# Transposing softmax probabilities on VectorE in 32 by 32 blocks instead of on TensorE, in a chunked attention fused with a squared-ReLU MLP

## The chip, the cores and the metric

The kernel runs on one core of a Trainium2 chip. The metric is device time in microseconds (us) of one launch; the time before is 877.12 us, the median of three runs (876.96 to 877.26).

The engines are named as in the profile: PE is TensorE's matmul stream and PEld its weight loads, DVE is VectorE, ACT is ScalarE, POOL is GpSimd, and SP is the engine that issues most DMAs.

## The reference

Attention is local: 8 batches by 8 heads, 576 positions, head size 64, cut into chunks of 64 positions that attend only within themselves. Its output, 4608 tokens by 512, feeds an MLP with a hidden size of 2048. All is float32.

```python
scores = (1/8) * q_c @ k_c.T            # per chunk: 64 x 64
attn = exp(scores - max(scores)); attn = attn / (sum(attn) + 1e-9)
x = attn @ v_c                          # gathered to tokens x 512
r = maximum(x @ w_in, 0)
out = (s * r * r + b) @ w_out
```

## The kernel before, in words

**Tiles.** The 4608 tokens are 36 tiles of 128. An MLP block (`Layer`) is four tiles, 512 tokens, so there are nine blocks; the attention for a block is done as two groups (`Attention`) of N = 2 tiles each. The hidden size is 16 slices of 128 (NJ = 16). Every float32 operand of the MLP is split into a high and a low part (`xh`/`xl`, `gh`/`gl`, and both halves of the weights), and each product is three matmuls.

**The steady loop** (lines 386 to 425) runs over j = 0 to 17 in every block. Step j issues `up(j)` (line 256, 12 matmuls 128x512 into one of two `ps_h` banks), then `square(j)` and `bias(j)`: ACT's relu (L263), DVE's product (L264, called the square here), ACT's `gh` (L269), DVE's `gl` (L270). Then comes `down(j-2)` (line 281, 12 matmuls into four `ps_o` banks): `LAG` is 2. `ps_h` has two buffers, so `up(j+2)` needs `gl(j)` done; `down(j)` needs both `gh(j)` and `gl(j)`.

**Attention inside the loop.** While block b's MLP runs, the attention of block b+1 is worked in at fixed places. `attention_plan` maps a place (j, phase) to steps: phase 0 stands ahead of `up(j)`, phase 1 behind it, phase 2 between `square(j)` and `bias(j)`. Every engine takes its instructions in this order; nothing reorders them (`manual_schedule`). A group has a base step n, 1 for the first and 9 for the second:

- (n-1, 0) loads, (n, 1) scores on PE (L171), (n, 2) maximum on DVE (L176)
- (n+1, 2) subtraction on DVE (L181), (n+2, 0) exp on ACT (L186), (n+2, 2) sum on DVE (L190)
- (n+4, 0) `norm`: three DVE instructions (L193 to L195)
- (n+5, 1) `transposes`: 8 PE transposes of 128x128 into PSUM (L202)
- (n+6, 0) `copies`: two ACT copies 128x512 from PSUM to `pT` (L207)
- (n+6, 1) `values`: 64 small matmuls with `pT` as the moving operand (L215)
- (n+7, 0) `x_hi` on ACT (L226), (n+7, 2) `x_lo` on DVE (L230); `x` is read by `up(0)` of the next block.

The scores, the transposes and the values take turns in one `ps_a` buffer of two PSUM banks. `p`, `pT`, `m` and `z` have one buffer each.

The attention of the first block is done in a prologue (lines 319 to 383), where the weights are also unpacked; `attention_plan(4)` supplies the second block's attention during the first block. The last block has no attention beside it. So `attention_plan` runs eight times, 16 groups in all, of which 14 have `tb` of 8 or more.

Of the kernel before, what the change touches and what calls it, by code (L numbers as in the profile page):

```python
# [1 line left out]

# [6 lines left out]
F32 = mybir.dt.float32  # L9
# [9 lines left out]
def local_attention_then_squared_relu_mlp(ctx: ExitStack, tc, qkv, w, s, b, out):  # L19


    nc = tc.nc
    P = 128
# [4 lines left out]
    NHP = H // 2  # L28
    LAG = 2
    N = 2  # L30
# [8 lines left out]
    att = ctx.enter_context(tc.tile_pool(name="att", bufs=1))  # L39
# [91 lines left out]
    class Attention:  # L131
# [65 lines left out]
        def transposes(self):  # L197
            p = self.p.rearrange("p g c k -> p g (c k)")
            self.ps = self.bank(1)
            for g in range(G):  # L200
                i, hp = divmod(g, NHP)
                nc.tensor.transpose(out=self.ps[:, i, hp * P:(hp + 1) * P], in_=p[:, g, :], identity=ident)  # L202

        def copies(self):
            pT = att.tile([P, N, NHP * P], F32, name="pT")
            for i in range(N):
                nc.scalar.copy(out=pT[:, i, :], in_=self.ps[:, i, :])  # L207
            self.pT = pT.rearrange("p i (a t) -> p i a t", a=NHP)
# [23 lines left out]
    def block(tb0, bank):  # L232
        x = [xp.tile([P, NHP, 4 * P], F32R, name=n) for n in ("xh", "xl")]
        return x, [Attention(tb0 + i, x, i * P, bank) for i in range(0, 4, N)]
# [73 lines left out]
    def attention_plan(tb0):  # L308
        x, groups = block(tb0, steady_bank)
        plan = {}  # L310
        for a, n in zip(groups, (1, 9)):
            for at, *fs in (((n - 1, 0), a.load_qk, a.load_v), ((n, 1), a.scores), ((n, 2), a.peak), ((n + 1, 2), a.sub),
                            ((n + 2, 0), a.exp), ((n + 2, 2), a.sum), ((n + 4, 0), a.norm), ((n + 5, 1), a.transposes),
                            ((n + 6, 0), a.copies), ((n + 6, 1), a.values), ((n + 7, 0), a.x_hi), ((n + 7, 2), a.x_lo)):
                plan.setdefault(at, []).extend(fs)
        return x, plan, plan.pop((0, 0))


    x, (one, two) = block(0, first_bank)
    for a in (one, two):  # L320
        a.p = wp.tile([P, 4, DM], F32, name="wp")[:, 0:2, :].rearrange("p i (g c k) -> p (i g) c k", g=NHP, c=2)
    next_x, plan, (load_next_qk, load_next_v) = attention_plan(4)
    pair = [Pair(k) for k in range(NJ)]
    one.load_qk()
# [61 lines left out]
    for tb0 in range(0, NTB, 4):  # L386
# [39 lines left out]
        previous, x, plan, loads = layer, next_x, {}, ()  # L426
        if tb0 + 4 < NTB:
            layer = Layer(tb0 + 4, x)
        if tb0 + 8 < NTB:
            next_x, plan, loads = attention_plan(tb0 + 8)  # L430
# [33 lines left out]
```

## Time and profile before

| | us |
|---|---|
| median of three runs | 877.12 (876.96 to 877.26) |
| the profiled execution's own time | 877.19 |
| its span (first to last instruction) | 875.4 |
| PE busy | 860.9 (98%) |
| DVE busy | 375.7 (43%) |
| ACT busy | 309.3 (35%) |
| POOL busy | 42.1 (5%) |
| mean granted TensorE clock | 0.998 of full |

The span plus 1.8 us makes the execution's own time. A matmul's busy time overlaps that of its neighbours, so the time of a matmul stream is read from start to start. The first block ends near 115 us of the span; from there on the eight others repeat one pattern.

### The profile page before, as it was taken

The numbers are of one execution on the slowest core, as the hardware profiler recorded it, in microseconds if no ns is written. First come the engines' busy times: TensorE is split into PE (matmuls) and PEld (weight loads), VectorE is DVE, ScalarE is ACT, GpSimd is POOL, SyncE is SP. The second block draws the span as 40 slices with busy tenths as digits, with TensorE's granted clock in tenths as the row PEclk, the third lists the DMA queues.
The fourth block names the chain that finished last, engine by engine and source line by source line (L and its number), as shares of the span: only waits on it lengthen the run. The fifth ranks groups of instructions, "written<-read, shape, count | busy, mean of one in ns | idle before, by whom it ended". The sixth has DMA issues, their size and how long they took to land.

```text
span 875.4 us, 13710 instructions
## 1 busy us (share of the span) xinstructions
PE 860.9 (98%) x5986; PEld 709.1 (81%) x5986; DVE 375.7 (43%) x486; ACT 309.3 (35%) x465; POOL 42.1 (5%) x24
## 2 busy tenths in 40 slices
PE   7899999999999999999999999999999999999998
PEld 6677888888888888888888888888888888888886
DVE  6898945242434333333434252443333343423222
ACT  5777643223322332223232332233222322232222
POOL 2434300000000000000000000000000000000000
PEclk9999999999999999999999999999999999999999
DMA  8556430201210030203020212002020300010001
GB/s 340 214 180 230 145 121 1 74 1 33 89 52 22 5 116 1 73 0 121 1 73 0 71 51 72 2 25 97 1 73 1 121 0 25 1 49 1 1 0 49
DMA packets 20368, 55.41 MB, mean 63 GB/s; under 512 B 2260, under 2 KB 2516, under 8 KB 20308
## 3 DMA queue, kind: packets, MB, share of 16 engines
q1 hardware_dynamic: 20160, 54.40, 17.6%
q8 instruction: 47, 0.77, 0.3%
q10 hardware_dynamic: 148, 0.13, 0.0%
q14 instruction: 13, 0.11, 0.0%
HBM read 45.09 MB, written 9.44 MB: 62 GB/s over the span
## 4 chain that ended last, share of the span: by engine, by line
PE 87%; DVE 6%; issue 2%; DMA 2%; ACT 2%; POOL 0%; SPq 0%; ACTq 0%; POOLq 0%
PE ps_o L281 42%; PE ps_h L256 40%; PE ps_a L215 2%; PE ps_a L171 2%; DVE wp L127 2%; DMA raw<-in_w_dram 2%; PE ps_a L202 1%; DVE ps_h L264 1%; DVE f L113 1%; DVE f L111 1%; DVE g L270 1%; ACT g L269 1%; ACT f L101 0%; DMA wp<-in_qkv_dram 0%; ACT raw L105 0%
## 5 line engine op out<-in xcount | busy, mean ns | idle before, releaser
L281 PE MATMUL ps_o<-wp,g 128*128 128x512 f32 x1728 | 417.0, 392 | 0.0
L256 PE MATMUL ps_h<-xh,wp 128*128 128x512 f32 (+1 forms) x1160 | 379.9, 390 | 4.5 <-DVE g L270 3.4
L281 PEld LDWEIGHTS ps_o<-wp,g 128*128 128x128 f32 x1728 | 321.3, 188 | 66.8
L264 DVE SCALAR_TENSOR_TENSOR ps_h<-ps_h,sb,r 128x512 f32<-128x512 f32 x144 | 109.1, 758 | 412.6 <-ACT r L263 412.4
L256 PEld LDWEIGHTS ps_h<-xh,wp 128*128 128x128 f32 x1160 | 217.5, 188 | 51.8 <-DVE g L270 3.5
L256 PE MATMUL ps_h<-xl,wp 128*128 128x512 f32 (+1 forms) x580 | 225.4, 389 | 0.0
L263 ACT ACTIVATE r<-ps_h 128x512 f32<-128x512 f32 x144 | 86.1, 598 | 373.1 <-PE ps_h L256 373.1
L269 ACT ACTIVATE g<-ps_h,sb 128x512 fp32r<-128x512 f32 x144 | 99.3, 689 | 118.2 <-DVE ps_h L264 118.2
L270 DVE SCALAR_TENSOR_TENSOR g<-ps_h,sb,g 128x512 fp32r<-128x512 f32 x144 | 107.6, 747 | 68.2 <-ACT g L269 68.2
L256 PEld LDWEIGHTS ps_h<-xl,wp 128*128 128x128 f32 x580 | 109.3, 189 | 22.2
L119 POOL TENSOR_TENSOR f<-f,raw 128x1024 int32<-128x1024 int32 (+1 forms) x17 | 39.5, 2321 | 67.8 <-DVE f L113 46.0
L298 ACT COPY f<-ps_o 128x512 f32<-128x512 f32 (+1 forms) x35 | 20.4, 583 | 41.4 <-PE ps_o L281 39.1
L101 ACT ACTIVATE f<-raw 128x1024 f32<-128x1024 f32 (+1 forms) x17 | 18.6, 1092 | 11.2 <-DMA raw<-in_w_dram 10.0
L113 DVE SCALAR_TENSOR_TENSOR f<-raw,f 128x1024 uint32<-128x1024 uint32 (+1 forms) x17 | 21.9, 1286 | 0.5
L127 DVE TENSOR_TENSOR wp<-f,wp 128x1024 fp32r<-128x1024 f32 (+1 forms) x17 | 22.0, 1292 | 0.0
L230 DVE TENSOR_TENSOR xl<-ps_a,xh 128x512 fp32r<-128x512 f32 x32 | 20.5, 683 | 1.7 <-ACT xh L226 1.7
L195 DVE TENSOR_TENSOR p<-p,z 128x1024 f32<-128x1024 f32 x16 | 19.6, 1225 | 0.6
L215 PEld LDWEIGHTS ps_a<-pT,v 64*64 64x64 f32 x960 | 15.4, 134 | 5.3 <-issue 4.9
L171 PEld LDWEIGHTS ps_a<-raw 64*64 64x64 f32 x960 | 15.4, 134 | 5.3 <-issue 5.3
L123 ACT CAST wp<-f 128x1024 fp32r<-128x1024 f32 (+1 forms) x17 | 16.9, 997 | 7.6 <-POOL f L119 7.5
L186 ACT ACTIVATE p<-p 128x1024 f32<-128x1024 f32 x16 | 17.0, 1063 | 6.9 <-DVE p L181 6.9
L181 DVE TENSOR_TENSOR p<-ps_a,m 128x1024 f32<-128x1024 f32 x16 | 19.4, 1215 | 0.0
(44 smaller groups left out, 238.7 us busy)
## 6 DMA issues: line engine op xcount, KB each, us to landing
raw<-in_w_dram SPq DMA_DIRECT2D x32, 512.0 KB, 4.6
raw<-in_qkv_dram SPq DMA_DIRECT2D x30, 512.0 KB, 4.7
out_dram<-f SPq DMA_DIRECT2D x35, 256.0 KB, 2.1
v<-in_qkv_dram SPq DMA_DIRECT2D x30, 256.0 KB, 3.1
wp<-in_qkv_dram SPq DMA_DIRECT2D x6, 512.0 KB, 6.0
wp<-in_qkv_dram SPq DMA_DIRECT2D x6, 256.0 KB, 7.6
out_dram<-f ACTq DMA_DIRECT2D x1, 128.0 KB, 2.1
out_dram<-f SPq DMA_DIRECT2D x1, 128.0 KB, 2.0
```

The costliest lines, as they stand in the source:

```text
L113: nc.vector.scalar_tensor_tensor(out=u, in0=high, scalar=0x80000000, in1=u, op0=ALU.bitwise_and, op1=ALU.bitwise_or)
L119: nc.gpsimd.tensor_tensor(out=i, in0=i, in1=low.bitcast(I32), op=ALU.add)
L127: nc.vector.tensor_tensor(out=lo, in0=f, in1=hi.bitcast(F32), op=ALU.subtract)
L171: nc.tensor.matmul(out=self.ps[cols, c, i * NHP + hp, :], lhsT=qk[rows, 0, h, :], rhs=qk[rows, 1, h, :], start=True, stop=True)
L215: nc.tensor.matmul(out=ps[i if apart else 0][cols, c, i * NHP + hp, :], lhsT=self.v[i][rows, h, :], rhs=self.pT[rows, i, hp, cols], start= ...
L230: nc.vector.tensor_tensor(out=lo, in0=ps, in1=hi.bitcast(F32), op=ALU.subtract)
L256: nc.tensor.matmul(out=self.ps[j][:, cols], lhsT=w[:, c, :], rhs=x[:, c, :], start=(c == 0 and i == 0), stop=(c == NHP - 1 and i == 2))
L263: nc.scalar.activation(out=r, in_=ps, func=AF.Relu)
L264: nc.vector.scalar_tensor_tensor(out=ps, in0=ps, scalar=s_col, in1=r, op0=ALU.mult, op1=ALU.mult)
L269: nc.scalar.activation(out=gh, in_=ps, func=AF.Identity, bias=b_col)
L270: nc.vector.scalar_tensor_tensor(out=gl, in0=ps, scalar=b_col, in1=gh.bitcast(F32), op0=ALU.add, op1=ALU.subtract)
L281: nc.tensor.matmul(out=self.acc[t], lhsT=x[:, ts], rhs=w, start=(j == 0 and i == 0), stop=(j == NJ - 1 and i == 2))
```

## The change

For groups with `tb` of 8 or more, the PE transposes at (n+5, 1) and the ACT copies at (n+6, 0) are gone. In their place VectorE transposes `p` into `pT` in sixteen instructions, each on 32 partitions by 8 blocks of 32 elements (256 elements in a row), from quarter t of the tokens to quarter k of the keys. Four are at (n+4, 2), six at (n+5, 0) and six at (n+5, 2). All other steps keep their places.

```diff
+        def turn(self, blocks):
+            if blocks[0] == 0:
+                self.pT = att.tile([P, N, NHP * P], F32, name="pT").rearrange("p i (a t) -> p i a t", a=NHP)
+            p = self.p.rearrange("p g c k -> p g (c k)")
+            for n in blocks:
+                t, k = (slice(32 * b, 32 * b + 32) for b in divmod(n, 4))
+                nc.vector.transpose(out=self.pT[k].rearrange("p i a t -> p (i a) t")[:, :, t], in_=p[t, :, k])
...
-                            ((n + 2, 0), a.exp), ((n + 2, 2), a.sum), ((n + 4, 0), a.norm), ((n + 5, 1), a.transposes),
-                            ((n + 6, 0), a.copies), ((n + 6, 1), a.values), ((n + 7, 0), a.x_hi), ((n + 7, 2), a.x_lo)):
+                            ((n + 2, 0), a.exp), ((n + 2, 2), a.sum), ((n + 4, 0), a.norm),
+                            ((n + 6, 1), a.values), ((n + 7, 0), a.x_hi), ((n + 7, 2), a.x_lo)):
                 plan.setdefault(at, []).extend(fs)
+
+            if a.tb < 8:
+                turns = ((n + 5, 1), a.transposes), ((n + 6, 0), a.copies)
+            else:
+                turns = [(at, partial(a.turn, range(*r))) for at, r in (((n + 4, 2), (0, 4)), ((n + 5, 0), (4, 10)), ((n + 5, 2), (10, 16)))]
+            for at, f in turns:
+                plan.setdefault(at, []).append(f)
```

## Rows read from the trace of the kernel before

**Rows 1.** Page, part 1: busy time of each engine, share of span, instructions
```profile
PE 860.9 (98%) x5986; PEld 709.1 (81%) x5986; DVE 375.7 (43%) x486; ACT 309.3 (35%) x465; POOL 42.1 (5%) x24
```

**Rows 2.** Chain that ended last, 115 to 875 us, by line
```profile
by line: PE ps_o L281 47.6%; PE ps_h L256 45.8%; PE ps_a L215 2.2%; PE ps_a L171 2.0%; PE ps_a L202 1.6%; DVE ps_h L264 0.1%; DVE g L270 0.1%; ACT g L269 0.1%; ACT r L263 0.1%; DVE f L296 0.1%; ACT f L298 0.1%; issue 0.0%; ACTq L263 0.0%
```

**Rows 3.** Waits, 115 to 875 us: total us, times, longest us
```profile
PEld ps_a L215 <- issue: 4.9, 14, 0.4
...
PEld ps_a L215 <- ACT pT L207: 0.4, 1, 0.4
PE ps_h L256 <- DVE g L270: 0.3, 1, 0.3
```

**Rows 4.** Groups of instructions by shape: the work removed (busy us, mean ns)
```profile
L207 ACT COPY pT<-ps_a 128x512 f32<-128x512 f32 x36 | 19.2, 590 | 0.0
...
L202 PE MATMUL ps_a<-ident,p 128*128 128x128 f32 x128 | 16.5, 272 | 0.0
```

**Rows 5.** Timeline, PE, a second group, steps 13 to 15: start us, us
```profile
288.90 0.39 PE L256 MATMUL ps_h<-xh,wp 128*128 128x512 f32 x1
...
294.34 0.39 PE L256 MATMUL ps_h<-xh,wp 128*128 128x512 f32 x1
...
297.06 1.03 PE L202 MATMUL ps_a<-ident,p 128*128 128x128 f32 x8
...
297.85 2.98 PE L281 MATMUL ps_o<-wp,g 128*128 128x512 f32 x12
...
300.67 0.39 PE L256 MATMUL ps_h<-xh,wp 128*128 128x512 f32 x1
...
303.48 1.16 PE L215 MATMUL ps_a<-pT,v 64*64 64x64 f32 x64
...
312.87 0.39 PE L256 MATMUL ps_h<-xh,wp 128*128 128x512 f32 x1
```

**Rows 6.** Timeline, PE, a first group, steps 6 and 7
```profile
341.39 0.39 PE L256 MATMUL ps_h<-xh,wp 128*128 128x512 f32 x1
...
347.72 0.39 PE L256 MATMUL ps_h<-xh,wp 128*128 128x512 f32 x1
```

**Rows 7.** Timeline, DVE, the same second group, steps 13 and 14 and behind them
```profile
289.25 0.16 DVE L193 TENSOR_SCALAR z<-z 128x16 f32<-128x16 f32 x1
289.45 0.25 DVE L194 RECIPROCAL z<-z 128x16 f32<-128x16 f32 x1
289.74 1.23 DVE L195 TENSOR_TENSOR p<-p,z 128x1024 f32<-128x1024 f32 x1
292.51 0.76 DVE L264 SCALAR_TENSOR_TENSOR ps_h<-ps_h,sb,r 128x512 f32<-128x512 f32 x1 [1.55 <-ACT r L263]
294.02 0.75 DVE L270 SCALAR_TENSOR_TENSOR g<-ps_h,sb,g 128x512 fp32r<-128x512 f32 x1 [0.76 <-ACT g L269]
297.95 0.76 DVE L264 SCALAR_TENSOR_TENSOR ps_h<-ps_h,sb,r 128x512 f32<-128x512 f32 x1 [3.18 <-ACT r L263]
299.47 0.75 DVE L270 SCALAR_TENSOR_TENSOR g<-ps_h,sb,g 128x512 fp32r<-128x512 f32 x1 [0.76 <-ACT g L269]
...
306.76 1.29 DVE L230 TENSOR_TENSOR xl<-ps_a,xh 128x512 fp32r<-128x512 f32 x2 [0.21 <-ACT xh L226]
```

**Rows 8.** Busy time in one stretch: PE, PEld, DVE, ACT, POOL, PEclk, DMA share, GB/s
```profile
287.86:303.40 15.54, 15.54 (x74) 12.75 (x72) 5.33 (x8) 4.23 (x7) 0.00 (x0) 1.00 0.00 0
```

**Rows 9.** Groups of instructions by shape: DVE durations, mean ns
```profile
L230 DVE TENSOR_TENSOR xl<-ps_a,xh 128x512 fp32r<-128x512 f32 x32 | 20.5, 683 | 1.7 <-ACT xh L226 1.7
...
L195 DVE TENSOR_TENSOR p<-p,z 128x1024 f32<-128x1024 f32 x16 | 19.6, 1225 | 0.6
L181 DVE TENSOR_TENSOR p<-ps_a,m 128x1024 f32<-128x1024 f32 x16 | 19.4, 1215 | 0.0
...
L127 DVE TENSOR_TENSOR wp<-f,wp 128x512 fp32r<-128x512 f32 x2 | 1.4, 681 | 0.0
...
L296 DVE COPY f<-ps_o 128x256 f32<-128x256 f32 x1 | 0.4, 425 | 1.1 <-ACT f L298 1.1
```

More of the change, by code (lines that the diff above doesn't have):

```diff
@@ L1 @@
 from contextlib import ExitStack
+from functools import partial
 import concourse.bass as bass
```

## The prediction

> **What bounds the kernel now.** I read the busy table first: PE is busy for 98% of the span, DVE for 43% [rows 1]. A busy PE need not be the bound, so next I read the chain that ended last, cut to the part behind the first block: its five PE lines sum to 99.2% [rows 2]. The transposes, L202, are 1.6% of that chain: they are part of the bounding stream, not beside it. Then the waits of the same stretch: in 760 us PE waits for another engine in two places, 0.4 and 0.3 us, and the only wait that repeats is 0.4 us of issue ahead of each set of values [rows 3]. So behind 115 us, time taken out of PE's stream comes off the end, as long as nothing new makes PE wait. Last I read one group's timeline, on PE for what the transposes cost and on DVE for the room there is.
>
> **The change, part by part.**
>
> *Removed from PE.* The page gives a transpose a mean of 272 ns [rows 4], but these overlap: the eight start at 297.06 and the next matmul at 297.85. The full cost is read from step to step. A step without attention takes 294.34 − 288.90 = 5.44 us; the step with the transposes takes 300.67 − 294.34 = 6.33 us [rows 5]. The difference is **0.89 us**. A first group has the same 347.72 − 341.39 = 6.33 us [rows 6]. The trace has 128 such transposes, 16 groups of eight [rows 4]; two groups (tiles 4 and 6) keep theirs by the condition on `tb`, so 14 lose them: 14 × 0.89 = **12.46 us**.
>
> *Removed from ACT.* Two copies of 590 ns per group [rows 4]. ACT waits for PE in these steps, and nothing on PE waits for ACT but the values, which have a new releaser. I cost it at zero, and it brings nothing more. Likewise `ps_a`: it changes hands twice a group instead of three times, but PE shows no wait on it [rows 3].
>
> *Added to DVE.* Sixteen transposes a group, of 256 elements in a row on 32 partitions. No row shows a VectorE transpose, so I bound its start-to-start time. Going from 512 to 1024 elements adds 1225 − 681 = 544 ns, so 256 elements would take 681 − 272 = 409 ns; the one copy of 256 elements took 425 [rows 9]. Short strided rows cost nothing by themselves: the subtraction writes `p` in runs of 64 and takes 1215 ns against the 1225 of the contiguous product [rows 9]. Independent neighbours overlap: the two pieces of `x_lo` together take 1.29 us where one takes 0.683, so the second starts some 0.08 us before the first ends [rows 7, 9]. Where each waits for the one before, as the three of `norm`, there is a gap of about 0.035 us instead [rows 7]. **Low end** 0.409 − 0.08 = 0.33 us, **usual high end** 0.425 + 0.035 = 0.46 us. An end far above that: should the transposing path take each float32 at half the rate, a row of 256 would cost what 512 cost, 0.683 + 0.035 = 0.72 us. I take 0.43, the duration of the 256-element copy with neither overlap nor gap, because its shape is the nearest.
>
> *The room for it.* The first four stand behind the square of step n+4, which ends at 292.51 + 0.76 = 293.27 [rows 7]. The values need the last; they start at 303.48 now, and would at 303.48 − 0.89 = 302.59 [rows 5]. In these 9.32 us DVE also does one `gl` (0.75) and one square (0.76) [rows 7]; four hand-offs of 0.035 make 0.14. That leaves 7.67 us, so sixteen transposes fit if one takes no more than **0.48 us**. At 0.43 they take 6.9 and 0.8 us is over; at 0.46 they take 7.4 and it still fits, by 0.3. In the stretch of the group's steps DVE is busy for 5.33 of 15.54 us [rows 8], and 6.9 more makes 12.2.
>
> *What is queued behind them.* On DVE the first four hold back `gl` of step n+4: it would start at 293.27 + 4 × 0.43 = 295.0 instead of 294.02. The six at (n+5, 0) then run to 295.0 + 0.75 + 2.6 = 298.35, and the square, ready at 297.95 now, waits 0.4 us for them [rows 7]. ACT's `gh` waits with it, and the last six then put `gl` of step n+5 to 298.35 + 0.76 + 2.6 = 301.7 instead of 299.47. Who needs that `gl`? The `down` two steps later, and `up` two steps later through the two `ps_h` buffers. In a first group that `up` starts two steps of 5.44 us behind the one at 294.34's place, after the values too: near 306. It has about 3.5 us to spare. In a second group the next block's `up(0)` stands at 312.87 [rows 5], and `x_lo` ends at 308.05 [rows 7], behind steps that are unchanged; DVE has caught up by then. I cost all these at zero: their cover is the LAG of two steps. The steps bring no DMA and pass neither SP's queue nor POOL's.
>
> *Sum.* 14 × 0.89 = 12.46 us off, nothing back. The profiled execution took 877.19, giving 864.73; against the median, 0.07 lower, it is **864.7 us**.
>
> The Trainium skill speaks against the change: "VectorE: DVE Perf Modes", section "Rules for kernel authors", says to transpose 128×128 on TensorE where a PSUM destination will do. By that rule alone the 12.46 us would not be had. The rows say why it need not hold here: PE is the chain and DVE idles for 10 us of the 15.54 [rows 2, 8].
>
> **The rivals.**
>
> *A thin stall.* The room is 0.48 us each, and my bounds reach 0.46. If the sixteen never overlap, and filling a block of 32 columns first adds 32/512 of 0.544, 0.034 us, one takes 0.425 + 0.035 + 0.034 = 0.494: the values wait 16 × 0.494 − 7.67 = 0.23 us a group, 3.3 us in all, giving **868.0**. With twice the gap, 0.529, the wait is 0.8 and the time 864.7 + 11.1 = 875.8, nearly all given back. For it: consecutive transposes go to another quarter of the partitions each time, a pattern that no row shows. Against: 512-element neighbours overlap. The skill's same page, section "Two Vector instructions with no wait between them", has a rule on the side of this rival: an instruction whose output or input starts in another group of 32 partitions than the last one's begins only when all earlier ones have finished. By it none of the overlap would be had; no run here shows it yet.
>
> *VectorE becomes the bound.* At half rate, 0.72 us each, sixteen take 11.5 us: the values wait 11.5 − 7.67 = 3.85 us in each of 14 groups, 54 us, giving **918.6 us**, slower. It decides from 0.48 + 0.89/16 = 0.54 us each, where the loss meets the gain. For it: nothing shows how fast float32 is transposed. Against: every DVE row is near one element per nanosecond, whatever its pattern [rows 9].
>
> *No gain from PE.* The removed 0.89 us might reappear as a wait for something else that was hidden behind it, at **877.1**. Against: PE has no wait of any size behind 115 us, and the square chain has whole steps to spare [rows 3, 7].
>
> **How the numbers follow.** All hidden, 864.7: chance 0.68. Thin stall, up to the 875.8 of the double gap: 0.17. No gain: 0.05. DVE the bound: 0.10. The likeliest is 864.7. Below it there is only the spread of single runs and the rounding of 0.89 (0.01 × 14), so the low end is 863.9. The high end takes in the thin stall at 0.494 and most of the way to the double gap, 871.5, which leaves out the two last cases and the worst of the second, under 0.2. About 0.2%, 1.75 us, is what a measurement of this kernel can tell from no change. Faster by more than that: the first case and nearly all of the second, 0.85; within it 0.05; slower 0.10.
>
> **What would show it.** Right: sixteen PE transposes of `p` left in place of 128; steps n+5 of 5.44 us in both groups; no wait of the values on DVE; a start-to-start time of the VectorE transposes under 0.48 us; DVE's busy time up by 14 × 16 × 0.43 = 96 us, PE's chain share still 99% behind the first block. Wrong: a wait of L215 on the VectorE transposes, repeated 14 times (thin stall under 0.9 us, DVE the bound above it); or a wait of `up` on `gl` at step n+7, which would show that I misjudged the cover of two steps.

## The result and the profile after

The changed kernel takes **864.60 us** (median of four runs, 864.37 to 865.99) against 877.04 in the same comparison: a ratio of 0.9859, 95% interval 0.9847 to 0.9872, or 12.4 us less. The forecast was 864.7. The profiled execution took 864.60 too, with a span of 862.8. One execution of the version below that starts the transposes earlier ran at a mean granted clock of 0.557 and took 1419.95 us; it is left out of that version's time.

The busy table, the chain behind the first block by line, and the waits there, of the changed kernel (the lines that answer to [rows 1 to 3]):

```profile
PE 847.9 (98%) x5874; PEld 697.2 (81%) x5874; DVE 472.2 (55%) x710; ACT 295.4 (34%) x437; POOL 42.1 (5%) x24
```

```profile
by line: PE ps_o L291 48.3%; PE ps_h L266 46.5%; PE ps_a L225 2.2%; PE ps_a L172 2.0%; DVE ps_h L274 0.1%; DVE g L280 0.1%; ACT g L279 0.1%; ACT r L273 0.1%; DVE f L306 0.1%; ACT f L308 0.1%; issue 0.0%; ACTq L273 0.0%
```

```profile
PEld ps_a L225 <- issue: 4.9, 14, 0.4
...
PEld ps_a L225 <- ACT pT L217: 0.4, 1, 0.4
PE ps_h L266 <- DVE g L280: 0.3, 1, 0.3
```

PE is as full as before, over a shorter span, and DVE's busy time has risen by 96.5 us, against the 96 that I had put. The chain has lost its 1.6% of transposes and gained nothing: the four PE lines sum to 99.0%. In the waits the row to look for is one that is not there: no wait of the values, now L225, for the VectorE transposes, L212 (the ACT row is the one group that keeps its copies). The three rows of before stand unchanged.

The two shapes that replace those of [rows 4], by shape and with the mean in ns:

```profile
L212 DVE STREAM_TRANSPOSE pT<-p 32x256 f32<-32x256 f32 x224 | 97.5, 435 | 3.9
...
L203 PE MATMUL ps_a<-ident,p 128*128 128x128 f32 x16 | 2.1, 272 | 0.0
```

The timeline of a second group, steps 13 to 15, on DVE (it answers to [rows 7]) and on PE ([rows 5]):

```profile
289.71 0.76 DVE L274 SCALAR_TENSOR_TENSOR ps_h<-ps_h,sb,r 128x512 f32<-128x512 f32 x1 [1.55 <-ACT r L273]
290.38 1.77 DVE L212 STREAM_TRANSPOSE pT<-p 32x256 f32<-32x256 f32 x4
292.19 0.75 DVE L280 SCALAR_TENSOR_TENSOR g<-ps_h,sb,g 128x512 fp32r<-128x512 f32 x1
292.97 2.70 DVE L212 STREAM_TRANSPOSE pT<-p 32x256 f32<-32x256 f32 x6
295.70 0.76 DVE L274 SCALAR_TENSOR_TENSOR ps_h<-ps_h,sb,r 128x512 f32<-128x512 f32 x1
296.49 2.71 DVE L212 STREAM_TRANSPOSE pT<-p 32x256 f32<-32x256 f32 x6
299.23 0.75 DVE L280 SCALAR_TENSOR_TENSOR g<-ps_h,sb,g 128x512 fp32r<-128x512 f32 x1
```

```profile
291.54 0.39 PE L266 MATMUL ps_h<-xh,wp 128*128 128x512 f32 x1
...
296.98 0.39 PE L266 MATMUL ps_h<-xh,wp 128*128 128x512 f32 x1
...
299.79 1.16 PE L225 MATMUL ps_a<-pT,v 64*64 64x64 f32 x64
300.89 3.47 PE L291 MATMUL ps_o<-wp,g 128*128 128x512 f32 x14
```

Step 14 takes 296.98 − 291.54 = 5.44 us, as one without attention did. In a first group the same step is 343.14 − 337.70 = 5.44 us:

```profile
337.70 0.39 PE L266 MATMUL ps_h<-xh,wp 128*128 128x512 f32 x1
...
343.14 0.39 PE L266 MATMUL ps_h<-xh,wp 128*128 128x512 f32 x1
```

On DVE everything from 289.71 to 299.98 stands in one row, with gaps of at most 0.04 us. The six of 2.70 us, the last of them 0.44 long, start every (2.70 − 0.44)/5 = 0.45 us. The last transpose ends at 296.49 + 2.71 = 299.20 and the values start at 299.79: **0.59 us of room**, little more than one transpose.

### The profile page after: what moved, and what is told of

It is laid out like the page before. It is cut to its first block, busy times and chain, and to the rows that moved or that the text cites. A ratio compares the mean times of both kernels' runs of the same rounds, so it can differ in the third digit from the quotient of the medians.

```text
span 862.8 us, 13668 instructions
## 1 busy us (share of the span) xinstructions
PE 847.9 (98%) x5874; PEld 697.2 (81%) x5874; DVE 472.2 (55%) x710; ACT 295.4 (34%) x437; POOL 42.1 (5%) x24
## 4 chain that ended last, share of the span: by engine, by line
PE 88%; DVE 7%; issue 2%; ACT 2%; DMA 1%; POOL 0%; SPq 0%; ACTq 0%; POOLq 0%
PE ps_o L291 42%; PE ps_h L266 41%; PE ps_a L225 2%; PE ps_a L172 2%; DVE wp L128 2%; DVE ps_h L274 1%; DVE f L114 1%; DVE f L112 1%; DVE g L280 1%; ACT g L279 1%; DMA raw<-in_w_dram 1%; DVE z L191 0%; PE ps_h L67 0%; DVE m L177 0%; POOL f L120 0%
## 5 line engine op out<-in xcount | busy, mean ns | idle before, releaser
L212 DVE STREAM_TRANSPOSE pT<-p 32x256 f32<-32x256 f32 x224 | 97.5, 435 | 3.9
L128 DVE TENSOR_TENSOR wp<-f,wp 128x1024 fp32r<-128x1024 f32 (+1 forms) x17 | 22.0, 1294 | 0.0
L225 PEld LDWEIGHTS ps_a<-pT,v 64*64 64x64 f32 x960 | 15.4, 134 | 5.3 <-issue 4.9
L177 DVE TENSOR_REDUCE m<-ps_a 128x16 f32<-128x1024 f32 x16 | 19.4, 1215 | 0.0
```

Of the source, the lines that this page charges most:

```text
L128: nc.vector.tensor_tensor(out=lo, in0=f, in1=hi.bitcast(F32), op=ALU.subtract)
L212: nc.vector.transpose(out=self.pT[k].rearrange("p i a t -> p (i a) t")[:, :, t], in_=p[t, :, k])
L225: nc.tensor.matmul(out=ps[i if apart else 0][cols, c, i * NHP + hp, :], lhsT=self.v[i][rows, h, :], rhs=self.pT[rows, i, hp, cols], start= ...
```

## The experiments

They were run in three lots, each beside the kernel before; a ratio is against that. Each is the changed kernel with the edit shown.

**Is the VectorE work hidden? Leave it out.** `pT` is filled with a constant instead, by one memset of 0.91 us a group.

```diff
-            for n in blocks:
...
+            if blocks[0] == 0:
+                nc.vector.memset(self.pT, 1.0 / CH)
```

> The sixteen VectorE transposes of a group are left out; pT is filled once per group with 1/64 by one memset, so the values are no longer those of the softmax. Theory (the transposes are wholly hidden behind TensorE): same time as the changed kernel, 864.6 us within 0.5. Rival (they still cost something, by holding back the squares or by stalling the values a little): lower by what they cost, 861 to 863.

Measured 864.54 us, ratio 0.9854 (0.9837 to 0.987). Sixteen transposes a group, 97.5 us of DVE time in the changed kernel's profile, cost nothing that can be measured.

**Is the gain PE's stream alone? Put the PE transposes back, unread.**

```diff
             else:
+                plan.setdefault((n + 5, 1), []).append(a.transposes)
```

> The changed kernel, with the eight TensorE transposes of each of the 14 groups put back at their old place; nobody reads them, no ScalarE copies follow. Theory (the gain is TensorE's stream alone): all of it is lost, 864.6 + 14 x 0.89 = 877.1 us. Rival (part of the gain came from the ScalarE copies that are gone and from the new releaser of the values): about half comes back, 868 to 874.

Measured 877.08 us, ratio 1.0001 (0.9991 to 1.001). The whole gain is gone. The two ScalarE copies and the new releaser of the values, both as in the changed kernel, are worth nothing; the rival with half of it falls. The third turn of `ps_a` came back together with the transposes, so this run does not part those two; neither trace shows a wait on it.

**How much room is there? Do one, two or four transposes twice.** The edit with two:

```diff
+                turns[2] = ((n + 5, 2), partial(a.turn, list(range(10, 12)) + list(range(10, 16))))
```

> One of the sixteen VectorE transposes of each group done twice (17 a group). Theory (0.55 us of room, 0.45 for one more): no stall, 864.6 us, and the last transpose ends some 0.1 us ahead of the values. Rival (two extra ones cost 5.3 us by a price each, not by a room): 2.7 us more, 867.3.

> Two of the sixteen VectorE transposes of each group are done twice (18 a group), ahead of the last six. Theory (the values have 0.5 to 0.6 us of room, one transpose takes 0.45): 2 x 0.45 - 0.55 = 0.35 us of stall a group, 14 of them, 869.5 us (868.5 to 870.5), with a wait of the values on the VectorE transposes. Rival (VectorE is idle for 45% of the span, so two more fit): 864.6.

> Four of the sixteen done twice (20 a group). Theory: 4 x 0.45 - 0.55 = 1.25 us a group, 17.5 us in all, 882 us, slower than the kernel before: the point from which VectorE decides is passed. Rival (they fit): 864.6; rival that the stall is taken up in the next steps: less than twice what two extra ones cost.

Measured 864.62 us with one (ratio 0.9858, 0.9843 to 0.9873), 869.94 with two (0.9917, 0.9902 to 0.9932) and 884.03 with four (1.0081, 1.0066 to 1.0096). The first is free, the next costs 5.3 us, and four turn the change into a loss. It is a room and not a price each: 0, 5.3 and 19.4 us for one, two and four.

With one extra, the last seven on DVE and the values on PE:

```profile
296.52 3.18 DVE L212 STREAM_TRANSPOSE pT<-p 32x256 f32<-32x256 f32 x7
...
299.82 1.16 PE L225 MATMUL ps_a<-pT,v 64*64 64x64 f32 x64
```

The last ends at 299.70, 0.12 us ahead of the values. With two, the last eight on DVE, the values and the matmul behind them on PE, and the wait that was missing above:

```profile
297.41 3.65 DVE L212 STREAM_TRANSPOSE pT<-p 32x256 f32<-32x256 f32 x8
```

```profile
300.72 1.54 PE L225 MATMUL ps_a<-pT,v 64*64 64x64 f32 x64
302.19 8.50 PE L291 MATMUL ps_o<-wp,g 128*128 128x512 f32 x36
```

```profile
PEld ps_a L225 <- DVE pT L212: 2.8, 14, 0.2
```

From the start of the values to the next matmul it is 302.19 − 300.72 = 1.47 us, where the changed kernel has 300.89 − 299.79 = 1.10. The difference of 0.37, 14 times, is 5.2 us: the measured loss. The wait row alone shows 2.8, so such a loss is read from start to start. With four, on PE:

```profile
305.62 0.80 PE L225 MATMUL ps_a<-pT,v 64*64 64x64 f32 x6
307.01 1.14 PE L225 MATMUL ps_a<-pT,v 64*64 64x64 f32 x58 [0.59 <-DVE pT L212]
308.08 4.19 PE L291 MATMUL ps_o<-wp,g 128*128 128x512 f32 x17
```

Here it is 2.46 us, 1.36 more than 1.10, and 14 × 1.36 = 19.0. I had expected 1.25; the values now stop twice, six of them ahead of the second stop. Which part of that makes the 0.1 us a group was not tried.

**Do neighbours overlap? Halve the transposes.** Each becomes two of 128 elements, one per tile, in the same quarters of the partitions.

```diff
-                nc.vector.transpose(out=self.pT[k].rearrange("p i a t -> p (i a) t")[:, :, t], in_=p[t, :, k])
+                for i in range(N):
+                    nc.vector.transpose(out=self.pT[k, i, :, t], in_=p[t, i * NHP:(i + 1) * NHP, k])
```

> Each VectorE transpose is done as two of 128 elements (one for each of the two tiles), one right after the other: both halves have the same quarter of the partitions for input and for output, the next pair another output quarter. Theory H (a transpose that starts in another quarter than its predecessor starts only when that has finished; neighbours in the same quarters overlap): the second half of a pair starts about 0.08 us before the first ends, the first half of the next pair 0.02 us after the end; a pair takes some 0.54 us, 16 pairs 8.7 us instead of 7.2, and the values wait 0.9 us a group: 877 us (873 to 881). Theory N (transposes never overlap, whatever the quarter): 32 x 0.32 = 10.2 us, a stall of 2.4 us a group, 898 us. Theory O (all overlap, the quarter has no part in it): 32 x 0.23 = 7.4 us, at most 867 us.

Measured 867.27 us (ratio 0.9888, 0.9873 to 0.9902): by the time alone, theory O. The trace says H. Four cuts of the DVE timeline, each wider than the one before it, show the first one, two, three and four of a row of halves (start of the first, us to the end of the last):

```profile
294.17 0.30 DVE L213 STREAM_TRANSPOSE pT<-p 32x128 f32<-32x128 f32 x1
...
294.17 0.49 DVE L213 STREAM_TRANSPOSE pT<-p 32x128 f32<-32x128 f32 x2
...
294.17 0.81 DVE L213 STREAM_TRANSPOSE pT<-p 32x128 f32<-32x128 f32 x3
...
294.17 1.00 DVE L213 STREAM_TRANSPOSE pT<-p 32x128 f32<-32x128 f32 x4
```

All of them, with the shortest, median and longest in ns:

```profile
L213 DVE STREAM_TRANSPOSE pT<-p x448: 256/278/307, 152.3 to 764.3; 32x128 f32<-32x128 f32 x150
```

The ends come alternately 0.19 and 0.32 us apart. The shortest lasts 256 ns, so the second of a pair starts at most 0.49 − 0.26 = 0.23 into the row, 0.07 or more before the first ends at 0.30; the third, which changes the output's quarter and takes 0.30, starts some 0.02 after the second ends. Same quarters overlap, other quarters don't. The Trainium skill states this in "VectorE: DVE Perf Modes", section "Two Vector instructions with no wait between them"; the trace agrees, with those 0.07 and 0.02 us. The changed kernel's own rows agree too: its first four transposes begin in the first quarter, where the square began, and start at 290.38, 0.09 before the square's end at 289.71 + 0.76 = 290.47; its last six begin in another quarter and start at 296.49, 0.03 behind the square's end at 296.46. A pair took 0.51 us where I had put 0.54, and the stall was not sixteen pairs against the room: the last half ends at 301.10 while the values had begun before it:

```profile
298.03 3.07 DVE L213 STREAM_TRANSPOSE pT<-p 32x128 f32<-32x128 f32 x12
```

```profile
300.76 1.34 PE L226 MATMUL ps_a<-pT,v 64*64 64x64 f32 x64
302.03 8.50 PE L292 MATMUL ps_o<-wp,g 128*128 128x512 f32 x36
```

302.03 − 300.76 = 1.27 is 0.17 more than 1.10, and 14 × 0.17 = 2.4 of the 2.7 us lost. The time agreed with the wrong theory because two sizes of the right one were off.

**Is a little stall left? Start earlier.**

```diff
-                turns = [(at, partial(a.turn, range(*r))) for at, r in (((n + 4, 2), (0, 4)), ((n + 5, 0), (4, 10)), ((n + 5, 2), (10, 16)))]
+                turns = [(at, partial(a.turn, range(*r))) for at, r in (((n + 4, 1), (0, 3)), ((n + 4, 2), (3, 6)), ((n + 5, 0), (6, 11)), ((n + 5, 2), (11, 16)))]
```

> The sixteen are spread as 3 at (n+4, 1), 3 at (n+4, 2), 5 at (n+5, 0) and 5 at (n+5, 2): the first three use VectorE's idle time ahead of the square of step n+4. Theory (the values already wait for nothing): 864.6 us, no gain, but the last transpose ends some 1.3 us earlier against the values. Rival (a little stall is left in the changed kernel): 862 to 864.

Measured 864.44 us (ratio 0.9855, 0.9839 to 0.9872). Its step 13 square and its last five transposes:

```profile
289.61 0.76 DVE L274 SCALAR_TENSOR_TENSOR ps_h<-ps_h,sb,r 128x512 f32<-128x512 f32 x1 [0.18 <-ACT r L273]
...
295.84 2.27 DVE L212 STREAM_TRANSPOSE pT<-p 32x256 f32<-32x256 f32 x5
```

The last ends at 298.11, with the square 0.10 earlier than in the changed kernel: 1.0 us more room (I had said 1.3), and no time gained. Nothing waits there.

**Can the attention worked into the first block go the same way?** Tiles 6 and 7 alone (`a.tb < 6`), then tiles 4 to 7 (`a.tb < 4`).

```diff
-            if a.tb < 8:
+            if a.tb < 6:
```

> The second group of the first plan (tiles 6 and 7, steps 13 to 15 of the first block) is transposed by VectorE too. If VectorE, which also unpacks weights there, has the room: 864.6 - 0.9 = 863.7 us. Rival (the unpacking of the last weights is held back and with it TensorE): 865 us or more.

> Both groups of the first plan are transposed by VectorE. If there is room in steps 5 to 7 too: 864.6 - 1.8 = 862.8 us. Rival (VectorE is the bound in the first block's middle, where it unpacks one pair of weights in each step): 7.2 us more VectorE work there moves the end by several us, 868 to 872.

Measured 869.32 us (ratio 0.9917, 0.9901 to 0.9934) and 873.18 (0.996, 0.9945 to 0.9974), 4.7 and 8.6 us more than the changed kernel. Six transposes and the instruction behind them on DVE, with tiles 6 and 7, then PE, then the same stretch of PE in the changed kernel:

```profile
111.32 2.68 DVE L212 STREAM_TRANSPOSE pT<-p 32x256 f32<-32x256 f32 x6
114.03 1.23 DVE L128 TENSOR_TENSOR wp<-f,wp 128x1024 fp32r<-128x1024 f32 x1
```

```profile
111.71 0.39 PE L266 MATMUL ps_h<-xl,wp 128*128 128x512 f32 x1
115.31 1.22 PE L266 MATMUL ps_h<-xh,wp 128*128 128x512 f32 x2 [3.22 <-DVE wp L128]
...
119.33 1.16 PE L225 MATMUL ps_a<-pT,v 64*64 64x64 f32 x64
```

```profile
112.57 0.39 PE L266 MATMUL ps_h<-xl,wp 128*128 128x512 f32 x1
112.80 0.62 PE L266 MATMUL ps_h<-xh,wp 128*128 128x512 f32 x2
...
115.15 1.16 PE L225 MATMUL ps_a<-pT,v 64*64 64x64 f32 x64
```

The low part of a weight (L128), which `up` needs next, is queued behind six transposes, and PE stands for 3.2 us: more than the 0.89 that the change gains. Then the granted clock (the last but two of each row) is lower for a while:

```profile
110.00:115.00 5.00, 2.10 (x10) 1.32 (x8) 4.82 (x10) 1.54 (x2) 0.82 (x1) 1.00 0.00 0
...
115.00:120.00 5.00, 4.69 (x54) 3.62 (x58) 4.85 (x10) 1.19 (x2) 0.00 (x0) 0.66 0.00 0
```

Behind a stretch with PE busy for 2.10 of 5.00 us the clock averages 0.66, between its two levels of 2.4 and 1.2 GHz; in the changed kernel it is 1.00 there. From start to start, the stop is 115.31 − 111.71 = 3.60 us where the changed kernel takes 0.23, so 3.4 lost; the rest of `up`, to the values, is 119.33 − 115.31 = 4.02 us where it takes 115.15 − 112.80 = 2.35, so 1.7 lost at the lower clock. Less the 0.9 gained, that is 4.2 us, which is what the two profiled executions differ by (868.80 − 864.60).

With tiles 4 to 7 a like stop comes earlier as well, again for a weight's low part behind six transposes:

```profile
66.63 0.74 PE L266 MATMUL ps_h<-xh,wp 128*128 128x512 f32 x2 [3.21 <-DVE wp L128]
```

The clock then averages 0.81 from 65 to 70 us and 0.50, which is 1.2 GHz, from 70 to 75; PE was busy for 3.42 of the 5.00 us from 60 to 65. What else makes up the 8.6 us was not worked out.

**A version to beat both?** For tiles 6 and 7 the last twelve transposes go behind that weight and the values one step later, with `x_hi` and `x_lo` behind them.

```diff
-                            ((n + 6, 1), a.values), ((n + 7, 0), a.x_hi), ((n + 7, 2), a.x_lo)):
+                            *((((n + 7, 1), a.values), ((n + 7, 2), a.x_hi, a.x_lo)) if a.tb == 6 else
+                              (((n + 6, 1), a.values), ((n + 7, 0), a.x_hi), ((n + 7, 2), a.x_lo)))):
...
-            if a.tb < 8:
+            if a.tb < 6:
...
+                turns = [(at, partial(a.turn, range(*r))) for at, r in ((((n + 4, 2), (0, 4)), ((n + 5, 2), (4, 10)), ((n + 6, 0), (10, 16))) if a.tb == 6 else
...
```

> The changed kernel once more, beside the next two on the same chip: 864.6 us, within 0.3.

> The second group of the first plan (tiles 6 and 7) is transposed by VectorE too, but later: four at (13, 2) as before, six at (14, 2) behind the weights' low part that TensorE waited for, six at (15, 0), and its values at (16, 1), x_hi and x_lo at (16, 2). Theory (what cost 4.7 us was the weight instruction queued behind six transposes, and the clock that fell after that stall): no stall, and 0.89 us less of TensorE: 863.7 us, ahead of both kernels. Rival (VectorE has no room in the first block at all, wherever they stand): 866 us or more.

Measured 864.58 us for the changed kernel again (ratio 0.9858, 0.9843 to 0.9873) and 866.28 for the late one (0.9878, 0.9861 to 0.9894). The stop of 3.2 us has shrunk, but the values now stop twice:

```profile
111.70 0.39 PE L266 MATMUL ps_h<-xl,wp 128*128 128x512 f32 x1
112.48 0.74 PE L266 MATMUL ps_h<-xh,wp 128*128 128x512 f32 x2 [0.39 <-DVE wp L128]
...
117.73 0.32 PE L225 MATMUL ps_a<-pT,v 64*64 64x64 f32 x2
118.58 0.33 PE L225 MATMUL ps_a<-pT,v 64*64 64x64 f32 x4 [0.52 <-DVE pT L212]
119.50 1.14 PE L225 MATMUL ps_a<-pT,v 64*64 64x64 f32 x58 [0.59 <-DVE pT L212]
120.57 5.72 PE L291 MATMUL ps_o<-wp,g 128*128 128x512 f32 x24
```

From start to start the weight's stop is 112.48 − 111.70 = 0.78 us, 0.55 more than the 0.23 of the changed kernel, and the values take 120.57 − 117.73 = 2.84 us, 1.74 more than 1.10. With 0.89 gained that makes 1.4 of the 1.7 us by which this version is slower; the rest was not traced. DVE (the third busy time of a row) has next to no idle time here:

```profile
104.00:112.00 8.00, 7.77 (x34) 5.78 (x32) 7.89 (x11) 3.00 (x5) 2.44 (x1) 1.00 0.00 0
112.00:118.00 6.00, 5.61 (x25) 4.24 (x24) 5.79 (x12) 1.68 (x3) 0.00 (x0) 1.00 0.00 0
```

It was late in both places tried; that it would be late wherever they stand is likely by these rows, but not shown. No version here is faster than the changed kernel by more than the spread of its runs.

## Why the prediction was right

*Removed from PE.* 0.89 us a group, read from step to step, times 14. The step is 5.44 us now, and the transposes put back cost 877.08 − 864.60 = 12.5 us. The mean of 272 ns a transpose would have given 2.2 us a group; start to start was the right reading.

*Removed from ACT,* and one turn less of `ps_a`: costed at zero. For the copies the same run shows it: without them and with the transposes the time is that of before. For `ps_a` it is argued: 14 × 0.89 leaves nothing of the 12.5 for it, and no wait on it stands in either trace.

*Added to DVE.* I took 0.43 us each between 0.33 and 0.46; it is 0.45. The duration, 435 ns, is the 425 of the 256-element copy and 10 more; the overlap that made the low end is not there, as a change of quarter excludes it. I had no row for that and held both ends open. No row of before could tell the 0.45 from the 0.494 of the thin stall, so that it stayed under the 0.48 was in part luck. And I read [rows 9] too kindly: near one element per nanosecond is only the slope from 512 to 1024 elements, 512 in 544 ns; the whole rows give 0.60 to 0.84, and the transpose 256/435 = 0.59.

*The room.* I worked out 7.67 us for sixteen, 0.48 each. Sixteen at 0.45 take 7.2, leaving some 0.5; the trace shows 0.59, as the first four start 0.09 ahead of the square's end. One more fits and two don't, as 0.59 against 0.45 and 0.90 says.

*What is queued behind them.* In the changed kernel's time, 2.80 us earlier here, my `gl` of step 13 at 295.0 is 292.2, and it starts at 292.19; the square of step 14 at 298.35 is 295.55, measured 295.70; `gl` of step 14 at 301.7 is 298.9, measured 299.23. PE has no wait on any of them that it had not before. (The waits of before hold two more rows than I named: 0.4 us of issue ahead of each set of scores too, and 0.8 us of weight loads on the one `gl`. Both stand unchanged in the changed kernel.)

*The rivals.* A thin stall like that of the first rival appears with eighteen transposes; a time above that of before, as the second rival has it, is reached with twenty, 884.03 us (nineteen were not tried). The rivals needed a transpose of over 0.48 and 0.54 us, and it takes 0.45. "No gain from PE" falls with the transposes put back. The rule of the Trainium skill that speaks for TensorE as the place of a 128×128 transpose ("VectorE: DVE Perf Modes", section "Rules for kernel authors") did not give the faster kernel here. VectorE takes 7.2 us for what cost TensorE 0.89, and it is still the better place, as it is hidden and TensorE is the chain.

## What to carry to other kernels

Moving work from the bounding engine to one that is slower at it paid here because it landed in that engine's idle time ahead of the first reader. So add up the engine's whole queue between the producer and that reader, not its mean load: 55% busy left room for one more transpose and not for two. The same move lost time in the one block where that queue was already full, through an instruction of another chain that stood behind it. Read both the gain and such a loss from start to start on the bounding engine; here the mean durations overstated the gain (2.2 us a group for 0.89), and the wait row understated the loss (2.8 us for 5.2).

## What the runs showed that I had not expected

In the prediction the quarter of the partitions stood only in a rival; the runs show that the start of the next VectorE transpose goes by whether it changes: 0.07 us before the end of the last one where it doesn't, 0.02 after it where it does. And a stall has a tail: with tiles 6 and 7 moved, PE's stop of 3.2 us was followed by a clock of 0.66 of full speed over the next 5 us, which cost another 1.7.
